# A DeltaNet layer and a multiplicative FFN in one kernel: feature products by 11 of 12 half products, two chunks transposed by TensorE

## The chip, the cores and the metric

One core of a Trainium2 chip runs the whole program. The metric is the device time of one execution in microseconds (us). Engines: TensorE (PE; its weight loads are listed as PEld), VectorE (DVE), ScalarE (ACT), GpSimd (POOL) and SyncE (SP), which issues nearly all transfers.

## What is computed

```
# attention, per (b, h), B=4, H=8, S=768, D=48
k_n = k / (norm(k) + 1e-6);  state = 0
for t in range(S):
    y[t]  = q[t] @ state
    state += beta[t] * outer(k_n[t], v[t] - k_n[t] @ state)
# x: 3072 tokens x 384, the heads side by side
a = x @ w1;  b = x @ w2          # 384 x 1024
out = ((a * b) @ w3) @ w_out     # 1024 x 1024, 1024 x 384
```

The first four inputs are float32. The weights arrive as float64 and are turned into float32 on the chip.

## The kernel before

**Attention.** The sequence is cut into 12 chunks (m) of 64 tokens. For a chunk the kernel loads k, v and q, brings k and q into feature order (`KQ`), forms scores (`scores`, step s), inverts a triangular 64x64 matrix per head from two 32-blocks, updates the state (`chain`, c) and writes the outputs, transposed, into `xT` (`outputs`, y), with six small transfers that move the last head pair's rows into place. Two neighbouring chunks make a pair j. The 32-blocks of a pair are inverted together by `inverse` (V): 31 steps of two DVE operations each, on `V` in PSUM for j < 2 and in SBUF from j = 2 on. `corner` (e) joins the blocks. `squares` (g) and `norms` (N) form the norms of k; their `across` takes a ps_f bank.

**Feature order.** Chunks 0 and 1 are transposed by TensorE (`by_tensor`, steps K and Q, L330, from the token buffers). Chunks 2 to 11 are loaded a second time, in pieces of 32 and 16 features, into `kperm` and `qperm` (`load_perm`, p, L223: 16 transfers each) and transposed by DVE in four operations (`by_vector`, d, L319).

**FFN.** It runs in six units u of 512 tokens, unit u on chunks 2u and 2u+1. First w3 and w_out are folded into `w34` (1024 x 384): `piece` (P, L695) loads a part of a weight into one of five `raw` buffers and turns it into float32 on ACT, DVE and POOL; `transpose_w3` (t) and `fold` (f, L756) do the product. The converted w_out (`wo`, L722) lies in the buffer of w2, so w2 is written after the folds. `ab` (a; b for the first half of unit 0) forms, for one tile of 128 features, x @ w1 and x @ w2 in one ps_f bank each, three matmuls of 512 columns each (L779); ACT copies the first (L791) and DVE multiplies with the second (L795) into a slab. There are ten slabs; a unit needs eight.

**Output.** The product of a unit's slabs (512 x 1024) with w34 is made by 7 instead of 8 block products: `weight_sums` (T) forms sums of blocks of w34 once, in raw buffers it keeps; `slab_sums` (S, L835) forms the sums of token and feature blocks of the slabs in place, on POOL, 16 operations of 128x256; `o` (L851) makes seven products of eight 192-column matmuls each into four ps_f banks named A, D, C, B; `result` (x, L901) adds them on ACT and DVE and stores. In the last unit two of the products go to other banks.

**Order.** `ORDER` lists the steps by name; every function is a generator that runs to its next `yield` when its name comes up. At the end `in_text_order` ties each engine's instructions to that order, so no engine overtakes its own list; between engines only data and buffers make waits. PSUM has four banks ps_f (`bank`) and two double banks ps_w (`two_banks`); both, and most SBUF buffers, are handed out in turn (`in_turn`).

Of the kernel before, what the change touches and what calls it, by code (L numbers as in the profile page):

```python
# [39 lines left out]
beta k0 P0 g0 P13 P10 P0 k1 P18 beta K0 P0 P0 P12 P13 P13 q0 P10 P18 P10 P10 K0 K0 P13 K0 beta  # L40
K0 g0 g0 q1 P8 P1 P18 g0 P12 P18 P12 K1 g0 k2 K1 K1 K1 g0 g0 P12 Q0 K1 Q0 Q0 g0 Q0 g0 P5 g0 N0
Q0 Q1 P8 P8 s0 t5 Q1 Q1 g1 Q1 Q1 s1 g1 s0 P8 g1 P9 s0 s1 s1 s1 s0 t4 t2 s0 p2 P1 P5 s0 s0 s1 s1
V0 P11 P5 P5 N0 P3 t5 P1 P1 d2 u0 P9 d2 u1 P11 P3 P9 P4 P11 N0 P3 t4 P4 P4 P9 P11 t3 t2 P2 P7
P2 P14 t0 P7 P3 P2 V0 V0 t10 P6 s1 P2 P14 t3 V0 P7 V0 V0 V0 P6 f1 g1 p3 P4 P7 t0 P14 P6 P6 P16
V0 V0 P15 V0 V0 V0 f2 V0 t10 P16 P16 f2 P15 f1 V0 f1 P16 P19 V0 V0 p2 t1 V0 P19 P19 V0 V0 f2 f0
P14 t6 t1 f0 f0 V0 P15 V0 P19 V0 v0 P15 t6 s1 P20 d2 V0 P17 P20 P20 t11 V0 P17 t11 d2 V0 t8 t8
P20 V0 k3 g1 g1 V0 g1 f5 P17 t7 V0 P17 V0 P22 P22 f5 V0 t7 V0 f5 v1 n0 V0 f3 V0 V0 s0 f3 P23
P26 V0 g1 f4 d3 t9 V0 t9 V0 d3 f4 P22 P22 f3 t14 P23 P23 P24 P24 P26 p3 t14 d3 f4 P23 n0 P30
P24 P24 s2 V0 p4 e0 g1 g1 t15 t12 f7 t15 f7 t12 f6 P26 P26 N1 e0 e0 s2 s2 P21 d3 e0 P30 e0 e0
s2 f7 s2 P25 e1 s2 c0 P21 e1 e1 e1 c0 n1 s3 P21 P21 N1 s3 y0 y0 P31 N1 s3 s3 s3 P25 P25 s3 n1  # L50
P31 c0 c0 P25 V1 P30 u2 t13 u3 P32 P30 V1 t13 e1 e1 c1 P31 V1 f6 f6 c1 c1 c1 y1 y0 b1 P32 P32
P32 y1 V1 V1 V1 b0 V1 P31 V1 b0 b2 V1 V1 b1 V1 V1 P27 P27 b1 V1 P27 V1 b1 b2 P29 P29 V1 b3 b3
P29 y1 b3 a03 V1 P28 V1 b3 P27 a01 a02 c1 a03 V1 a00 V1 k4 V1 P29 P28 P28 a01 a00 V1 V1 a00 P28
a02 a05 a00 V1 b5 V1 a05 b6 V1 V1 V1 V1 P35 p4 P35 b6 P33 a07 V1 V1 V1 V1 V1 V1 g2 a07 a04 b5
a04 b7 P33 k5 a06 b4 b7 v2 n2 a01 V1 P35 P33 a06 P34 a03 c1 V1 a03 V1 b2 V1 P35 P33 g2 P34 P34
P34 e2 b2 a01 c2 d4 d4 g2 p5 b4 b0 a04 d4 g2 g2 b0 g2 g2 e2 a07 a06 g2 g2 a04 d4 e2 n2 c2 a07
V2 b4 a06 e2 e2 e2 b5 c2 g2 N2 s4 c2 b4 S0 s4 s4 a02 a02 c2 c2 p5 T b5 T y2 b6 y2 d5 T b7 d5 d5
e3 e3 d5 N2 s4 s4 s4 N2 b7 e3 e3 v3 a05 T u4 a05 s5 b6 S0 s5 s5 S0 s5 s5 n3 o0 x0 e3 e3 s5 c3
n3 c3 S0 u5 S0 S0 S0 S0 o0 S0 S0 S0 S0 c3 c3 o0 V2 y3 x0 o0 V2 S0 V2 S0 V2 V2 V2 o0 V2 y3 V2 k6
x0 S0 g3 c3 g3 g3 S0 g3 V2 v4 x0 o0 V2 V2 V2 y3 V2 a10 a10 x0 x0 k7 x0 o0 V2 x0 x0 a17 V2 V2 V2  # L60
V2 x0 V2 V2 V2 a17 V2 V2 a15 V2 V2 a13 a16 V2 V2 v5 V2 a13 p6 V2 a16 V2 a15 V2 g3 V2 a13 g3 a13
p6 x0 a14 c3 a14 V2 e4 d6 a10 a17 a12 e4 e4 e4 g3 g3 c4 a17 g3 d6 a10 a14 d6 a12 n4 n4 c4 e4 g3
e4 e5 n5 a12 c4 a11 d6 N3 a14 c4 c4 n5 a11 y4 p7 p7 c4 e5 s6 a11 s6 s6 y4 a15 a12 a11 c5 e5 V3
a16 d7 d7 d7 d7 o1 c5 v6 a16 k8 g4 g4 e5 g4 p8 a15 g4 s7 s7 S1 e5 s7 S1 e5 x1 s7 s7 S1 s7 c5 o1
s6 S1 u7 c5 o1 s6 s6 u6 S1 S1 V3 S1 y5 c5 c5 V3 V3 V3 V3 V3 o1 S1 x1 k9 S1 y5 S1 y5 o1 S1 S1 x1
x1 V3 S1 S1 V3 c6 V3 S1 S1 V3 d8 o1 x1 x1 v7 a20 n6 x1 V3 a20 o1 x1 a23 V3 V3 x1 V3 x1 n7 a27
a24 d8 a26 V3 V3 V3 V3 x1 g4 V3 a23 V3 a25 V3 a27 a27 V3 a24 V3 V3 a26 a20 V3 g4 V3 p8 V3 V3 V3
V3 p9 V3 V3 a25 d8 n6 d8 g4 a20 a22 a22 a24 V3 c6 a27 a25 a24 a21 a21 e6 e6 e6 g4 e7 N3 e6 a25
N3 g4 s8 g4 N4 s8 e6 a22 s8 a26 e6 c6 c6 N4 s8 a26 s8 y6 a22 V4 p9 N4 S2 d9 e7 s8 a21 e7 y6 u8
d9 a21 e7 c6 a23 d9 p10 e7 d9 S2 c6 S2 s9 n7 a23 s9 e7 o2 s9 c7 s9 S2 s9 k10 S2 c7 x2 o2 c7 S2  # L70
S2 o2 u9 s9 V4 c7 V4 S2 y7 V4 V4 x2 V4 g5 g5 V4 p10 d10 y7 S2 x2 S2 o2 y7 V4 o2 x2 c7 V4 V4 S2
S2 V4 o2 a35 x2 x2 k11 x2 S2 V4 x2 S2 a35 v8 V4 S2 V4 V4 S2 V4 x2 n8 o2 a37 x2 V4 v9 V4 V4 V4
x2 a34 n8 V4 V4 a36 a30 V4 V4 V4 V4 V4 a37 V4 a34 a33 V4 g5 a33 a30 a32 a36 V4 V4 V4 V4 a34 a33
V4 V5 a32 e8 n9 c7 e8 a30 c8 a33 e8 e9 e8 g5 a35 a34 c8 a30 e8 g5 d10 a32 e9 g5 a32 g5 a36 e8
e9 S3 c8 a36 a35 a31 d10 d10 e9 a31 n9 c8 g5 c8 c8 g5 g5 e9 a31 s10 N5 e9 p11 s10 s10 a31 c9
# [14 lines left out]
def kernel(  # L90
# [24 lines left out]
    NT = 2 * B * C  # L115
    assert (B, H, D, DM, NT) == (4, 8, 48, 384, 512) and NCH % 2 == 0

# [74 lines left out]
    kperm, qperm = (padded(x, [P, B, NP, 2, BS], 1)[0] for x in ("kperm", "qperm"))  # L192
# [30 lines left out]
    def load_perm(m):  # L223
        for src, dst in ((k, kperm), (q, qperm)):
            for e in range(2):
                for j in range(2):
                    nd = min(BS, D - BS * j)
                    for tb in range(2):
                        t0 = C * m + BS * tb
                        sync.dma_start(  # L230
                            out=dst[quarter(2 * e + j), :, :, tb, 0:nd].rearrange(
                                "t b a d -> t (b a) d"
                            ),
                            in_=src.rearrange("b (a e) t d -> e (b a) t d", e=2)[
                                e, :, t0 : t0 + BS, BS * j : BS * j + nd
                            ].rearrange("g t d -> t g d"),
                        )
            yield
# [7 lines left out]
    def across(src, dst):  # L246

        n = src.shape[1]
        ps = bank([P, n, NR, NP])
# [3 lines left out]
        psv = ps[:].rearrange("p c r a -> p (c r) a")  # L253
# [10 lines left out]
    def squares(j):  # L264
# [9 lines left out]
        yield from across(ss[:, 1], ss[:, 0])  # L274

    def norms(j):
# [31 lines left out]
        yield from across(w[:, 0], w[:, 1])  # L308
# [10 lines left out]
    def by_vector(m):  # L319
        KQ = new_KQ(m)  # L320
        for i, src in enumerate((kperm, qperm)):
            for z in range(2):
# [3 lines left out]
                    in_=src[:, bs].rearrange("p b a x d -> p (b a) (x d)"),  # L326
# [363 lines left out]
    CW = 512  # L690

    def slab(name):
        return in_turn(ffn, [P, CW], "slab", 10, name)

# [27 lines left out]
    wo = w2s[:].rearrange("p m f -> p (m f)").rearrange("p (j d) -> p j d", d=DM)  # L722

    def piece_wo(j):
        return piece(DM, [(slice(0, P), moe_w_out[j * P : (j + 1) * P, :])], lambda: wo[:, j])
# [30 lines left out]
    def fold(jc):  # L756
        ps = bank([P, CW])
        for kc in range(KF):
            pe.matmul(  # L759
                ps[:, 0:DM], lhsT=w3Ts[jc, kc // 4][:, kc % 4 * P : kc % 4 * P + P],  # L760
                rhs=wo[:, kc], start=(kc == 0), stop=(kc == KF - 1),
# [38 lines left out]
    HB, HF, HD = B // 2, KF // 2, DM // 2  # L800
    ws_ = {}
# [4 lines left out]
    def weight(i):  # L806
        f, d = i
        return w34[:, HF * f : HF * f + HF, d_half(d)]

    def weight_sums():  # L810
# [11 lines left out]
        U3 = room[4][:, 0:DM]  # L822
        ws_.update(T1=B12, T2=T2, T3=T3, T4=T4, B11=B11, B21=B21, B22=B22, M1=M1, U2=U2, U3=U3)
# [10 lines left out]

    def slab_sums(u):  # L835
        for out_, x, y, op in (
# [5 lines left out]
            for i in range(HF):  # L842
                o_, x_, y_ = (
                    abs_[u, HF * f + i][:, tokens(z)] for z, f in (out_, x, y)
                )
                pool.tensor_tensor(out=o_, in0=x_, in1=y_, op=op)  # L846
                yield
# [3 lines left out]
    def o(u):  # L851
        for z, f, w, n, first in (
# [18 lines left out]
            for b in range(HB):  # L871
                t0 = (HB * z + b) * P
                for i in range(HF):
                    pe.matmul(  # L874
                        ps[b][:, b, :], lhsT=abs_[u, HF * f + i][:, t0 : t0 + P],
# [20 lines left out]
    last = NCH // 2 - 1  # L896
# [4 lines left out]
    def result(u):  # L901
# [17 lines left out]
        else:  # L919
            plus("M1", "B")(ws_["U3"])  # L920
            yield
        yield from store(u, 1, 1, plus("U3", "C"))
        yield from store(u, 1, 0, plus("U3", "D", ALU.subtract))
# [6 lines left out]
    def load_k(m, dma=sync.dma_start):  # L930
        ktoks[m] = load_crossed(k, m, dma, "ktok", 4)
# [32 lines left out]
    parts = {"beta": betas_, "T": weight_sums}  # L964
# [11 lines left out]
    for m in range(2):  # L976
# [3 lines left out]
    for j in range(NCH // 2):  # L980
# [3 lines left out]
        for jc in range(KF):  # L984
            parts[f"a{j}{jc}"] = lambda u=j, jc=jc: ab(u, jc, u == 0, 2)
        if j == 0:
            for jc in range(KF):
# [57 lines left out]
```

## Time and profile before

| | us |
|---|---|
| median of 3 runs | 609.24 |
| lowest, highest | 608.55, 610.59 |
| span of the profiled execution | 607.4 |
| PE busy, PEld busy | 550.0, 383.1 |
| DVE, ACT, POOL busy | 364.9, 158.9, 177.2 |

The span is the time from the first to the last instruction of one profiled execution; the runs' times are taken around whole executions. In the groups of the profile a row names line, engine, operation, out<-in by the program's names, shapes and count, then busy us and the mean ns of one, then the idle time ahead and what ended it. A float32 matmul stands as two rows of TensorE, two passes. PEclk is the share of TensorE's clock that was granted. A wait is put down to the last of its releasers.

### The profile page before, as it was taken

How to read it: one execution, taken by the hardware profiler on the slowest of the kernel's cores; microseconds unless marked ns; L12 is line 12 of the kernel's file. 1: busy time of each engine (PE TensorE's matmuls, PEld its weight loads, DVE VectorE, ACT ScalarE, POOL GpSimd, SP SyncE). 2: the span in 40 equal slices, each digit the busy share in tenths (PEclk: the TensorE clock that was granted, in tenths of full speed). 3: DMA queues.
4: the chain of work that ended last, by engine and by line, in shares of the span. 5: the costliest groups of instructions: out<-in, count | busy, mean ns of one | idle time of the engine just before them, and what ended most of it. 6: DMA issues, size and time to landing. Idle time of an engine off the chain costs nothing.

```text
span 607.4 us, 19078 instructions
## 1 busy us (share of the span) xinstructions
PE 550.0 (91%) x8188; PEld 383.1 (63%) x8188; DVE 364.9 (60%) x828; ACT 158.9 (26%) x333; POOL 177.2 (29%) x223
## 2 busy tenths in 40 slices
PE   2648789678898999999999989999999999999997
PEld 2545455657777885456964559745588545984477
DVE  3768977466998489765489463894764843311012
ACT  3645534445323111222111221121112012321100
POOL 6554443122255530304420016013053000600041
PEclk9988979669999999999999999999999999999999
DMA  9968998554956347462443534435323040010001
GB/s 192 244 155 226 186 189 173 97 133 94 165 104 88 82 92 120 92 98 39 101 101 73 81 52 87 97 70 103 58 51 84 31 85 5 5 52 13 1 0 52
DMA packets 219507, 57.31 MB, mean 94 GB/s; under 512 B 206656, under 2 KB 212800, under 8 KB 219424
## 3 DMA queue, kind: packets, MB, share of 16 engines
q1 hardware_dynamic: 215232, 55.31, 45.3%
q10 hardware_dynamic: 4192, 0.79, 0.9%
q8 instruction: 64, 1.05, 0.8%
q14 instruction: 19, 0.16, 0.1%
HBM read 43.88 MB, written 11.01 MB: 90 GB/s over the span
## 4 chain that ended last, share of the span: by engine, by line
PE 75%; DVE 8%; DMA 5%; issue 4%; ACT 3%; SPq 3%; ACTq 0%; DVEq 0%
PE ps_f L779 37%; PE ps_f L874 16%; PE ps_w L551 5%; PE ps_f L759 4%; PE ps_w L652 4%; DMA raw<-in_moe_w_dram 3%; PE ps_w L498 3%; PE ps_w L367 2%; DVE tb L440 2%; PE ps_w L373 2%; SPq L230 2%; DVE ps_w L445 2%; DMA ktok<-in_k_dram 1%; ACT xT L673 1%; PE ps_f L750 1%
## 5 line engine op out<-in xcount | busy, mean ns | idle before, releaser
L779 PE MATMUL ps_f<-xT,w2s 128*128 128x512 f32 (+1 forms) x336 | 133.7, 544 | 1.6 <-issue 1.5
L779 PE MATMUL ps_f<-xT,w1s 128*128 128x512 f32 (+1 forms) x336 | 128.7, 533 | 4.5 <-DVE ab L795 2.0
L846 POOL TENSOR_TENSOR ab<-ab 128x256 f32<-128x256 f32 x96 | 67.2, 729 | 195.0 <-DVE ab L795 171.0
L779 PEld LDWEIGHTS ps_f<-xT,w1s 128*128 128x128 f32 x336 | 63.0, 190 | 60.3 <-issue 52.0
L779 PEld LDWEIGHTS ps_f<-xT,w2s 128*128 128x128 f32 x336 | 63.2, 193 | 56.2 <-issue 52.3
L791 ACT COPY ab<-ps_f 128x512 f32<-128x512 f32 (+1 forms) x56 | 28.4, 525 | 172.7 <-PE ps_f L779 161.4
L874 PE MATMUL ps_f<-w,ab 128*128 128x192 f32 x376 | 66.5, 330 | 0.0
L874 PEld LDWEIGHTS ps_f<-w,ab 128*128 128x128 f32 x376 | 61.1, 190 | 4.4 <-issue 3.5
L795 DVE TENSOR_TENSOR ab<-ab,ps_f 128x512 f32<-128x512 f32 (+1 forms) x56 | 33.2, 605 | 49.1 <-PE ps_f L779 49.0
L440 DVE TENSOR_TENSOR tb<-Vb,Ub 128x31 f32<-128x31 f32 (+15 forms) x124 | 46.0, 371 | 15.5 <-DMA Ub<-Ud 12.1
L759 PE MATMUL ps_f<-w2s,w3T 128*128 128x384 f32 x128 | 48.4, 535 | 5.7 <-ACT w3T L753 5.0
L445 DVE TENSOR_TENSOR Vb<-Vb,tb 128x31 f32<-128x31 f32 (+15 forms) x124 | 47.2, 381 | 4.3
L874 PE MATMUL ps_f<-room,ab 128*128 128x192 f32 x272 | 47.9, 330 | 1.1 <-DVE room L905 1.1
L874 PEld LDWEIGHTS ps_f<-room,ab 128*128 128x128 f32 x272 | 44.1, 190 | 1.9 <-issue 1.5
L673 ACT COPY xT<-ps_w 48x256 f32<-48x256 f32 x96 | 30.4, 365 | 48.1 <-PE ps_w L652 47.5
L759 PEld LDWEIGHTS ps_f<-w2s,w3T 128*128 128x128 f32 x128 | 26.2, 211 | 24.2 <-ACT w3T L753 5.5
L270 POOL TENSOR_TENSOR sq<-ktok 128x384 f32<-128x384 f32 x24 | 20.9, 875 | 61.4 <-DMA ktok<-in_k_dram 30.1
L367 PE MATMUL ps_w<-KQ 48*64 48x128 f32 x384 | 31.3, 308 | 3.9 <-issue 2.0
L379 DVE TENSOR_TENSOR U<-ps_w,wt 128x512 f32<-128x512 f32 x24 | 16.6, 690 | 29.9 <-PE ps_w L373 28.6
L715 POOL TENSOR_TENSOR w<-w,raw 128x512 uint32<-128x512 uint32 x16 | 20.7, 1299 | 43.6 <-DVE w L711 18.6
L373 PE MATMUL ps_w<-KQ 48*64 48x64 f32 x768 | 32.1, 242 | 0.3 <-issue 0.3
L537 POOL TENSOR_TENSOR vtok<-vtok,n 128x384 f32<-128x384 f32 x24 | 20.1, 851 | 41.0 <-DMA vtok<-in_v_dram 26.8
(109 smaller groups left out, 676.4 us busy)
## 6 DMA issues: line engine op xcount, KB each, us to landing
raw<-in_moe_w_dram SPq DMA_DIRECT2D x16, 512.0 KB, 6.2
vtok<-in_v_dram SPq DMA_DIRECT2D x24, 192.0 KB, 4.3
raw<-in_moe_w_dram SPq DMA_DIRECT2D x24, 192.0 KB, 4.0
out_dram<-osb SPq DMA_DIRECT2D x46, 96.0 KB, 2.2
ktok<-in_k_dram SPq DMA_DIRECT2D x44, 96.0 KB, 3.9
raw<-in_moe_w_out_dram SPq DMA_DIRECT2D x8, 384.0 KB, 4.8
Ud<-U SPq DMA_DIRECT2D x48, 64.0 KB, 2.1
Ub<-Ud SPq DMA_DIRECT2D x6, 512.0 KB, 3.4
```

Of the source, the lines that this page charges most:

```text
L367: pe.matmul(ps[half(z), 0, n : n + 128], lhsT=x[:, 0, :], rhs=x.rearrange("p j t -> p (j t)"), start=True, stop=True,)
L373: pe.matmul(ps[half(z ^ j), 1, n + C * j : n + C * j + C], lhsT=x[:, 0, :], rhs=x[:, j, :], start=True, stop=True,)
L440: dve.tensor_tensor(out=tv, in0=V[:, 0 : s + 1, s : s + 1].to_broadcast([P, s + 1, n]), in1=U[:, s, s + 1 : BS].unsqueeze(1).to_broadcast( ...
L445: dve.tensor_tensor(out=o, in0=o, in1=tv, op=ALU.subtract)
L551: pe.matmul(out(ps, r, h, z), lhsT=lhs(r, h, z), rhs=rhs(r, h, z), start=True, stop=True,)
L673: act.copy(out=xT[f, p:NP:2, b : b + NR, cc, :].rearrange("p a r t -> p r a t"), in_=pyv[f, z, b : b + NR],)
L759: pe.matmul(ps[:, 0:DM], lhsT=w3Ts[jc, kc // 4][:, kc % 4 * P : kc % 4 * P + P], rhs=wo[:, kc], start=(kc == 0), stop=(kc == KF - 1),)
L779: pe.matmul(ps[:].rearrange("p b c t -> p b (c t)"), lhsT=w[:, m, js], rhs=x[:, m, :, c0:c1].rearrange("p b c t -> p b (c t)"), start=(m = ...
L791: act.copy(out=t, in_=ps)
L795: dve.tensor_tensor(out=t, in0=t, in1=ps, op=ALU.mult)
L846: pool.tensor_tensor(out=o_, in0=x_, in1=y_, op=op)
L874: pe.matmul(ps[b][:, b, :], lhsT=abs_[u, HF * f + i][:, t0 : t0 + P], rhs=ws_[w][:, i], start=first and i == 0 and (b == 0 or n == "F"), s ...
```

## The change

1. **Feature products of units 1 to 5.** The two halves of a unit's 512 tokens are the block rows. Of the 384 inputs, the first two tiles of 128 are the block columns; w1 and w2 are the block columns on the other side. These 2x2x2 block products are made by 7 instead of 8; the third tile of 128 adds its 4 as they are. `features` (steps a1x to a5x, now four a unit, each for two feature tiles) replaces `ab` there and makes the eleven half products in four ps_f banks; `features_sums` (W) forms the weight sums once, `token_sums` (X) the token sums of a unit, partly in the fourth slot of `xT`, partly in a new buffer `extra`. `tmp` and `first` are new single buffers between ACT, POOL and DVE. Slabs hold two feature tiles of one token half; there are nine.
2. **slab_sums** works on these slabs, eight operations of 128x512; in the last unit on DVE.
3. **Chunks 2 and 3** are transposed by TensorE (`range(4)` for `range(2)`); their q is loaded by tokens.
4. **One permuted buffer** `perm` serves k and then q for chunks 4 to 11; the new buffer `more` holds two blocks of w_out and later a weight sum.
5. **w_out** lies in the second `xT` buffer (five blocks), in `more` (two) and in `tmp` (one).
6. `ktok` has three buffers instead of four; `across` takes ps_w from pair 2 on; `result` keeps a sum in M1 instead of U3 except in the last unit.
7. **ORDER** is new, 1595 steps for 1317. The feature steps of unit 2 and their surroundings, before and after:

```
 before: ... a20 ... a23 V3 V3 x1 V3 x1 n7 a27 / a24 d8 a26 V3 V3 V3 V3 x1 g4 V3 a23 V3 a25 ...
 after:  ... x1 x1 n6 n6 a20 V3 V3 X2 X2 / X2 X2 S1 S1 o1 S1 c6 p8 d8 d8 x1 x1 N3 x1 x1 x1 p8 V3 V3 V3 S1 o1 x1 x1
         a20 V3 V3 V3 V3 n7 V3 V3 / n7 N3 V3 V3 a20 a20 a20 ... d8 / c6 a21 a21 a21 ...
```

```diff
-    kperm, qperm = (padded(x, [P, B, NP, 2, BS], 1)[0] for x in ("kperm", "qperm"))
+    perm = padded("perm", [P, B, NP, 2, BS], 1)[0]
+    more = persist.tile([P, 2 * CW], FP32, name="more")
+    tmp, first = (persist.tile([P, 2, C * B], FP32, name=x) for x in ("tmp", "first"))
+    extra = persist.tile([P, C * B], FP32, name="extra")
...
-        return in_turn(ffn, [P, CW], "slab", 10, name)
+        return in_turn(ffn, [P, CW], "slab", 9, name)
...
-    wo = w2s[:].rearrange("p m f -> p (m f)").rearrange("p (j d) -> p j d", d=DM)
+    def wo(j):
...
+            x = in_turn(ffn, [P, NP, B, 2, C], "xT", 2, "wo")
...
+        host, i = (guests[0], j) if j < 5 else (more, j - 5)
+        if j == 7:
+            host, i = tmp[:].rearrange("p j t -> p (j t)"), 0
+        return host[:, DM * i : DM * i + DM]
...
+    def token_sums(u):
+        A11, A12, A21, A22 = (x_of(u, i % 2, i // 2) for i in range(4))
+        S1, S2, S3 = A21, x_of(u, KM, 1), x_of(u, KM, 0)
+        for out_, x, y, op in (
+            (S3, A11, A21, ALU.subtract),
+            (S1, A21, A22, ALU.add),
+            (S2, S1, A11, ALU.subtract),
+            (extra[:], A12, S2, ALU.subtract),
+        ):
+            pool.tensor_tensor(out=out_, in0=x, in1=y, op=op)
+            yield
...
+        def onto(ps, w, x, first=False):
+            for j in range(2):
+                pe.matmul(
+                    ps[:, j, :], lhsT=w[j], rhs=x, start=first and j == 0, stop=j == 1,
+                    skip_group_check=not first,
+                )
...
+        ps_a = new()
+        onto(ps_a, B11, A11, True)
+        yield
+        Y0 = both(slab("y0"))
+        act.copy(out=Y0, in_=ps_a[:])
+        yield
+        ps_b = new()
+        onto(ps_b, T1, S1, True)
+        yield
+        act.copy(out=tmp[:], in_=ps_b[:])
+        yield
+        ps_d = new()
+        onto(ps_d, T2, S2, True)
+        yield
+        dve.tensor_tensor(out=Y0, in0=Y0, in1=ps_d[:], op=ALU.add)
+        yield
+        pool.tensor_tensor(out=tmp[:], in0=tmp[:], in1=Y0, op=ALU.add)
+        yield
+        ps_c = new()
+        onto(ps_c, T3, S3, True)
+        yield
+        Y1 = both(slab("y1"))
+        dve.tensor_tensor(out=Y1, in0=Y0, in1=ps_c[:], op=ALU.add)
+        yield
+        onto(ps_a, B21, A12)
+        yield
+        onto(ps_a, B31, X1)
+        yield
+        act.copy(out=first[:], in_=ps_a[:])
+        yield
+        onto(ps_b, B22, S4)
+        yield
+        onto(ps_b, B32, X1)
+        yield
+        dve.tensor_tensor(out=Y0, in0=Y0, in1=ps_b[:], op=ALU.add)
+        yield
+        pool.tensor_tensor(out=Y0, in0=Y0, in1=first[:], op=ALU.mult)
+        yield
+        onto(ps_d, T4, A22, True)
+        yield
+        onto(ps_d, B31, X2)
+        yield
+        dve.tensor_tensor(out=Y1, in0=Y1, in1=ps_d[:], op=ALU.add)
+        yield
+        onto(ps_c, B32, X2)
+        yield
+        dve.tensor_tensor(out=tmp[:], in0=tmp[:], in1=ps_c[:], op=ALU.add)
+        yield
+        pool.tensor_tensor(out=Y1, in0=Y1, in1=tmp[:], op=ALU.mult)
+        abs_[u, p, 0], abs_[u, p, 1] = Y0, Y1
+        yield
...
-                pool.tensor_tensor(out=o_, in0=x_, in1=y_, op=op)
+                (dve if u == last else pool).tensor_tensor(out=o_, in0=x_, in1=y_, op=op)
...
-    for m in range(2):
+    for m in range(4):
         parts[f"q{m}"] = lambda m=m: load_q(m, act.dma_start if m == 0 else sync.dma_start)
```

## The prediction, before the changed kernel was run

> **What bounds the kernel now.** I read the page first, parts 1, 2 and 4.
>
> ```profile
> span 607.4 us, 19078 instructions
> PE 550.0 (91%) x8188; PEld 383.1 (63%) x8188; DVE 364.9 (60%) x828; ACT 158.9 (26%) x333; POOL 177.2 (29%) x223
> PE   2648789678898999999999989999999999999997
> DVE  3768977466998489765489463894764843311012
> PEclk9988979669999999999999999999999999999999
> DMA  9968998554956347462443534435323040010001
> PE ps_f L779 37%; PE ps_f L874 16%; PE ps_w L551 5%; PE ps_f L759 4%; PE ps_w L652 4%; DMA raw<-in_moe_w_dram 3%; PE ps_w L498 3%; PE ps_w L367 2%; DVE tb L440 2%; PE ps_w L373 2%; SPq L230 2%; DVE ps_w L445 2%; DMA ktok<-in_k_dram 1%; ACT xT L673 1%; PE ps_f L750 1%
> ```
>
> Two regimes: up to about slice 9 no engine is full, DMA is busiest and the clock falls; afterwards PE is full. The chain that ended last is PE for 75%, the feature products (L779) alone 37%. So I asked the windows view for seven stretches, cut at unit 0's first product and at the last product of each unit's o step (columns: stretch, its length, busy time of PE, PEld, DVE, ACT, POOL, PEclk, DMA share, GB/s).
>
> ```profile
> 0.00:139.30 139.30, 98.41 (x1565) 71.15 (x1565) 93.09 (x202) 65.51 (x122) 59.69 (x68) 0.87 0.81 177
> 139.30:232.30 93.00, 86.20 (x1471) 73.44 (x1472) 73.45 (x179) 27.59 (x66) 37.10 (x45) 0.98 0.54 102
> 232.30:313.30 81.00, 79.33 (x1366) 53.09 (x1365) 54.77 (x122) 15.27 (x34) 19.99 (x28) 1.00 0.53 92
> 313.30:393.80 80.50, 77.81 (x1245) 51.32 (x1244) 52.91 (x128) 15.36 (x34) 16.77 (x24) 1.00 0.44 76
> 393.80:472.70 78.90, 78.66 (x1305) 52.03 (x1304) 51.30 (x120) 15.18 (x34) 21.35 (x29) 1.00 0.39 76
> 472.70:546.50 73.80, 72.75 (x1042) 47.07 (x1041) 30.33 (x64) 15.08 (x34) 11.18 (x16) 1.00 0.14 35
> 546.50:607.40 60.90, 56.86 (x203) 35.04 (x201) 9.08 (x16) 4.96 (x9) 11.10 (x16) 1.00 0.05 16
> ```
>
> In the last five PE works 365.4 of 375.1 us; 4.1 of the idle 9.7 is the tail after the last product. What PE saves there is saved, if nothing else becomes late. In the first stretch 41 us of PE lie idle.
>
> **Part 1, the products of units 1-5.** A matmul stands as two passes. From the chain and the PE timeline:
>
> ```profile
> 546.54 38.62 PE ps_f L779 x90
> 585.16 13.00 PE ps_f L874 x80
> 143.21 1.46 PE L779 MATMUL ps_f<-xT,w2s 128*128 128x256 f32 x6
> 144.51 1.46 PE L779 MATMUL ps_f<-xT,w1s 128*128 128x256 f32 x6
> 145.80 1.46 PE L779 MATMUL ps_f<-xT,w2s 128*128 128x256 f32 x6
> ```
>
> A 512-wide pass takes 38.62/90 = 0.429 us. At 256 wide six passes start 1.295 apart, 0.216 a pass; at 192 wide 0.1625. Two feature tiles now cost 12 matmuls x 2 x 0.429 = 10.30 us; after, 11 half products x 2 matmuls x 2 x 0.216 = 9.50. Saved: 0.80 x 20 pairs = **16.0 us of PE**. Weight loads rise from 24 to 44 a pair, 190 ns each = 8.4 us; they stay hidden, since in the 192-wide stretch one stands behind every 162 ns pass (they overlap each other). The Trainium skill (Perfetto Trace Analysis, Matmuls) says that larger matmuls are more efficient than smaller ones, which speaks against halving them; here the half-width pass costs 50.3% of a full one, so by the rows the penalty is 0.06 us a pair, and that is in the sum. If halving cost the whole saving, the sum below would be 16 higher, 608.
>
> **Part 2, what the saved product costs elsewhere**, per pair of tiles. DVE: five 128x512 operations with a PSUM operand for two (row L795, 682 ns): +2.05 us, +41 in all. POOL: three 128x512 operations of SBUF (row L393, 1276 ns): +3.8, +77 in all. ACT: three copies for two (587 ns), +12 in all. Once a unit POOL forms token sums, 4 x 0.73 = 2.9; once, weight sums, 6 x 1.28 + 4 x 0.73 = 10.6. Slab sums become 8 x 1.28 = 10.2 for 16 x 0.73 = 11.7 in units 1-4; in unit 5 eight move to DVE, about 0.69 each = 5.5. DVE ends near 405 us, POOL near 263, so neither is full by its sum. Stretch by stretch, counting what stands between the same marks in the new order at before's durations: PE 73.9 in unit 0 (72.8 by the same count before), then 74.7, 74.7, 73.5, 69.1, 58.0 = 350.0 for units 1-5 (before 365.4); DVE 86, 67, 58, 52, 38 for units 0 to 4. DVE has room from unit 2 on; in units 0 and 1 it has little.
>
> **Part 3, the hand-overs.** One pair uses all four ps_f banks. In the new PE order the tightest are d and c: DVE must have read the bank within two half products, 1.73 us; one read is 0.68 plus about 0.2 of signalling. So a pair runs dense when DVE is free and misses when a longer operation stands ahead (R, S: 0.95). Between the sixth and seventh product of an o step two DVE operations (2 x 0.55, with signals 1.5) stood behind a 2.57 us feature product; after, behind 0.86: 0.65 late, each unit. A missed wait costs about 0.3, as at 176.6 to 178.1, where four passes took 1.46 instead of 0.86 over two waits. I take 2.6 us a unit, 13 for five, from 0 (all hidden) to 35 (every second half product misses: 5.5 x 0.3 x 20 = 33). One spare slab instead of two, and single tmp, first and extra: tmp passes DVE, POOL and ACT (0.9 + 1.4 + 0.8 = 3.1) while PE does five half products (4.3); hidden. The copy that waits there holds ACT's queue, with y's copies and the corners' behind it, for which only the chunks wait. Units 1-5 then are 350.0 + 4.1 + 13 = 367 for 375.1: **-8**.
>
> **Part 4, the head.** Chunks 2 and 3: four groups of 64 passes, 1.95 to 2.4 us each (L337), +8.8 on PE, in its 41 idle us; if that cover were gone, +8.8 on the path. DVE loses eight transposes (0.69) and gains four copies (0.67): -2.8; ACT +12 x 0.58. SP loses 32 issues of about 0.62 and gains 4. Each chunk's 8192 small packets (16 transfers of 32 x 16 rows) become 2048 for q's tokens (k's are loaded either way); at the mean of part 3 (45.3% x 607.4 x 16 / 215232 = 20.5 ns, on 16 engines) that is 10.5 us for 2.6, at most 16 for both, of 113 busy. The q loads go to token buffers that Q0 and Q1 have freed; k3 now waits for chunk 0's state product and holds SP, but stands behind that product in the order. w_out in xT frees w2s for w2 before the folds end; w2's first half landed in time anyway (no idle before the first L779 on w2s), so 0. One buffer for k and q makes q's loads wait for k's transposes; SP already waited 12.8 us on such (L230 on DVE), the bound here is another 12.8, of which I take 0, since two chunks' worth has gone.
> The chain: k, scores, V0 (31 steps of DVE), corner 0, chunks 0 and 1, first product at 139.3. V0 began at 52.7, 14 us after the last U, its load standing on SP behind chunk 2's k; 28 us of DVE work stood ahead of it, after 23. It ended at 84.9, but corner 0's transpose came at 104.0, behind norms, w1 and w3 pieces; after, six w3 pieces (6.7 us) stand there. What was pushed back (norms, scores, 17 us) now stands between chunks 0 and 1. To the end of chunk 1 DVE has 98 us for 106. I take **-9** for the first stretch, between 0 and -18 (V0 10 earlier, 8 less work). Unit 0 keeps its 93: PE unchanged, DVE 86 of it.
>
> **The sum.** 130.3 + 93 + 367 = 590.3 against the span of 607.4. The median of the runs, 609.24, is 1.8 above that span; 590.3 + 1.8 = **592**.
>
> **Rivals.**
> A, DVE shut out by POOL. In the timeline around the end of unit 1 (start, length, engine, operation):
>
> ```profile
> 311.90 0.41 DVE L445 TENSOR_TENSOR Vb<-Vb,tb 128x240 f32<-128x240 f32 x1
> 312.70 0.83 POOL L537 TENSOR_TENSOR vtok<-vtok,n 128x384 f32<-128x384 f32 x1 [14.20 <-DMA out_dram<-osb]
> 312.80 1.00 DVE L445 TENSOR_TENSOR Vb<-Vb,tb 128x247 f32<-128x247 f32 x1
> ```
>
> With both inputs in SBUF, DVE ended only after POOL did; L795, which reads PSUM, stays at 0.68. V2 to V5 are 248 such operations, and in the new order they stand in the o phases beside slab sums, token sums and v's scaling: 8 x 1.28 + 4 x 0.73 + 2 x 0.85 = 14.9 us a unit. DVE's room is 7 us in unit 0 and 8 in unit 1, then 17 and 22: 8 + 7 = 15 us late, 592 + 15 = 607, from 600. For it: DVE's load; against: before, 24 of the 248 were lengthened, by 0.35 us on the mean, 8 us, since POOL was mostly done first. The Trainium skill (GPSIMD Engine Reference, Key points) has the two sharing SBUF interfaces for DVE instructions with two SBUF inputs; the rows agree. Chance 0.17.
> B, the other side: the banks. If DVE, behind 0.4 to 0.95 us of other work, misses d, c and four more of the eleven hand-overs, each costs 0.3 plus about 0.2 waited: 6 x 0.5 x 20 = 60 us of PE instead of 13, 592 + 47 = 639; it decides from 3 misses a pair (30 us, 609) on, so 611 to 640. For it: every bank is in use, and 20 pairs have no fifth. Against: covers of 1.7 us and more. The Trainium skill (TensorE: Matmul & The Clock Gate, A second HAM failure mode) says that cycling through PSUM with small idles can drop the clock as well; here the clock stayed at 1.00 through the last five stretches. Chance 0.22.
> C, the head gains nothing (another chain, raw loads or DVE's order, is as late): 592 + 9 = 601. Chance 0.08.
> D, the head gains all 18 and the hand-overs cost nothing: 592 - 9 - 13 = 570, half way 581. Chance 0.13.
> That the change does not do what it says: the instruction counts show 440 half-width products for 240, so I leave it out.
>
> **How the numbers follow.** The forecast (585 to 600) has 0.40. Faster by over 0.3%, about what a measurement of this kernel can tell from no change: 0.40 + D 0.13 + C 0.08 + 0.10 of A = 0.71; within: 0.07 of A; slower: B, 0.22. The range 582 to 616 leaves out about 0.06 of D and 0.12 of B.
>
> **What would show it.** Right: L779's successors at 0.216 a pass in runs of many; stretches of 77 to 79 us for units 1 and 2; first unit-0 product near 130; L465 at its 0.4. Wrong: PE idle before feature products on DVE's y or tmp (B); L460 and L465 near 1 us in the o phases (A); DVE above 95% in units 0 and 1, so that they do not shorten.

## The result, and the profile after

The changed kernel takes 659.17 us (median of 4 runs, 654.25 to 661.5) beside 608.89 for the kernel before (605.83 to 610.59). The ratio is 1.083, 95% interval 1.078 to 1.088: **slower by 8%**, where 592 was forecast and 616 was the upper end. The profiled execution took 654.25 us, the least of the four; its stretches below account for 45 of the 50 us.

The page of the changed kernel, parts 1, 2 and 4:

```profile
span 652.3 us, 20578 instructions
PE 556.6 (85%) x8844; PEld 472.6 (72%) x8844; DVE 457.9 (70%) x892; ACT 177.9 (27%) x365; POOL 263.0 (40%) x264
DVE  2789966788777898668987487985586796403352
PEclk9857998798995979999969998999999899999999
PE ps_f L920 20%; DVE tb L460 9%; PE ps_f L1028 9%; DVE Vb L465 8%; PE ps_f L807 4%; PE ps_w L571 4%; DMA raw<-in_moe_w_dram 2%; PE ps_w L518 2%; PE ps_w L672 2%; PE ps_w L387 1%; PE ps_w L393 1%; SPq L717 1%; DVE w L729 1%; DMA ktok<-in_k_dram 1%; PE ps_f L357 1%
```

POOL ends at 263.0 us, as forecast; DVE at 457.9 instead of 405. In the chain stand the two operations of V (L460, L465) with 17% of the span; before, they had 4%. The granted clock dips far behind the head. The windows view, cut at the same marks as before (first unit-0 product, last product of each o step; columns as in the prediction):

```profile
0.00:124.65 124.65, 90.19 (x1489) 64.08 (x1489) 90.71 (x187) 69.97 (x130) 57.28 (x66) 0.84 0.81 180
124.65:248.20 123.55, 103.10 (x1869) 88.43 (x1866) 100.78 (x202) 29.94 (x70) 54.00 (x60) 0.88 0.50 88
248.20:344.07 95.87, 79.01 (x1386) 68.89 (x1385) 76.41 (x143) 17.74 (x38) 36.26 (x34) 0.95 0.42 75
344.07:432.03 87.96, 79.98 (x1385) 70.52 (x1385) 66.83 (x136) 17.74 (x38) 35.79 (x33) 0.96 0.42 76
432.03:517.17 85.14, 77.43 (x1317) 67.66 (x1317) 59.06 (x114) 17.64 (x38) 36.33 (x35) 0.98 0.37 69
517.17:593.04 75.87, 71.48 (x1125) 62.50 (x1125) 40.97 (x75) 17.52 (x38) 28.11 (x24) 1.00 0.14 32
593.04:652.30 59.26, 55.43 (x284) 50.50 (x283) 23.17 (x36) 7.41 (x13) 15.24 (x12) 1.00 0.05 17
```

Against before the head is 14.6 us shorter. Unit 0 is 30.5 longer, unit 1 14.9, unit 2 7.5, unit 3 6.2, unit 4 2.1; unit 5 is 1.6 shorter. The loss shrinks from unit to unit with DVE's load, and unit 5, which has no V beside it, is the only one that gains.

**Where PE waits.** TensorE's timeline in unit 1's o phase (start, length, engine, line, what; in brackets idle time and releaser):

```profile
319.78 2.76 PE L1028 MATMUL ps_f<-room,y 128*128 128x192 f32 x16
322.38 1.03 PE L920 MATMUL ps_f<-xT,w1s 128*128 128x256 f32 x4
335.67 4.23 PE L1028 MATMUL ps_f<-room,y 128*128 128x192 f32 x16 [12.27 <-DVE room L1058]
341.23 2.84 PE L1028 MATMUL ps_f<-w,y 128*128 128x192 f32 x16 [0.17 <-DVE osb L1058]
```

The fifth product (319.78) opens bank B. DVE must read it (L1058) before the sixth adds to it. This read is the fourth step of `result`; outside the lists of the order x3 and x4 stand for the third and fourth step of one unit's result, so the read is called x4. DVE came to it at 334.98:

```profile
334.98 0.55 DVE L1058 TENSOR_TENSOR room<-room,ps_f 128x384 f32<-128x384 f32 x1
```

PE stood for 12.27 us; the sixth product then took 4.23 us instead of 2.8, at half clock. The same wait is 6.50 us in unit 0 (the profile names POOL there, but the product starts 0.15 us after DVE's read ends), 4.26, 4.32 and 0.81 in units 2 to 4: 28.2 us, and 7 more in four products at half clock. In unit 3 DVE itself stood idle for 4.98 us ahead of V5, waiting for a transfer (Ub from Ud), so there the wait is not DVE's work alone. Waits of feature products (L920) come to 6 us in all.

**What DVE does meanwhile.** DVE's timeline at the start of that phase, and POOL's:

```profile
307.82 1.26 DVE L465 TENSOR_TENSOR Vb<-Vb,tb 128x31 f32<-128x31 f32 x1
309.12 1.22 DVE L460 TENSOR_TENSOR tb<-Vb,Ub 128x60 f32<-128x60 f32 x1
311.60 0.25 DVE L460 TENSOR_TENSOR tb<-Vb,Ub 128x87 f32<-128x87 f32 x1
```
```profile
307.77 1.27 POOL L976 TENSOR_TENSOR y<-y,tmp 128x512 f32<-128x512 f32 x1 [2.26 <-DVE tmp L974]
309.00 5.22 POOL L1000 TENSOR_TENSOR y<-y,y 128x512 f32<-128x512 f32 x4
```

A DVE operation on 31 elements a partition takes 1.26 us and ends just after POOL's; the one at 311.60, which slipped in between two of POOL's, takes 0.25. So **about one operation of V passes for each operation of POOL**. Over the run, V2 to V5 take 128.3 us for 93.2.

The o phase of unit 1, first to last product, before and after, in the windows view (columns as above), and of the same windows the larger V row each (busy us, mean ns):

```profile
281.70:313.30 31.60, 30.56 (x648) 27.77 (x647) 19.88 (x45) 5.26 (x13) 11.79 (x17) 1.00 0.43 90
```
```profile
309.30:344.10 34.80, 22.37 (x186) 21.64 (x186) 31.56 (x52) 4.09 (x11) 16.56 (x16) 0.85 0.28 53
```
```profile
L445 DVE TENSOR_TENSOR Vb<-Vb,tb 128x31 f32<-128x31 f32 (+12 forms) x13 | 4.8, 371 | 0.4
```
```profile
L465 DVE TENSOR_TENSOR Vb<-Vb,tb 128x192 f32<-128x192 f32 (+14 forms) x23 | 14.3, 623 | 0.8
```

Before, this phase held 26 operations of V (9.0 us with L440) beside 30.6 us of PE work, a chunk's scores among it. Now it holds 46 of V (28.5 us with L460), and PE has little but o's products. PE's and DVE's work no longer lie side by side.

### The profile page after: what moved, and what is told of

Same layout as the page of the kernel before. It is cut to its first block, busy times and chain, and to the rows that moved or that the text cites. A ratio compares the mean times of both kernels' runs of the same rounds, so it can differ in the third digit from the quotient of the medians.

```text
span 652.3 us, 20578 instructions
## 1 busy us (share of the span) xinstructions
PE 556.6 (85%) x8844; PEld 472.6 (72%) x8844; DVE 457.9 (70%) x892; ACT 177.9 (27%) x365; POOL 263.0 (40%) x264
## 4 chain that ended last, share of the span: by engine, by line
PE 46%; DVE 30%; issue 7%; DMA 6%; SPq 5%; ACT 3%; POOL 1%; DVEq 0%; POOLq 0%; ACTq 0%
PE ps_f L920 20%; DVE tb L460 9%; PE ps_f L1028 9%; DVE Vb L465 8%; PE ps_f L807 4%; PE ps_w L571 4%; DMA raw<-in_moe_w_dram 2%; PE ps_w L518 2%; PE ps_w L672 2%; PE ps_w L387 1%; PE ps_w L393 1%; SPq L717 1%; DVE w L729 1%; DMA ktok<-in_k_dram 1%; PE ps_f L357 1%
## 5 line engine op out<-in xcount | busy, mean ns | idle before, releaser
L920 PE MATMUL ps_f<-xT,w1s 128*128 128x256 f32 x320 | 79.8, 382 | 0.7 <-DMA xT<-xT 0.7
L465 DVE TENSOR_TENSOR Vb<-Vb,tb 128x31 f32<-128x31 f32 (+15 forms) x124 | 65.7, 530 | 4.3
L460 DVE TENSOR_TENSOR tb<-Vb,Ub 128x31 f32<-128x31 f32 (+15 forms) x124 | 62.6, 505 | 8.2 <-DMA Ub<-Ud 5.0
L920 PEld LDWEIGHTS ps_f<-xT,w1s 128*128 128x128 f32 x320 | 60.0, 190 | 9.0 <-issue 1.0
L920 PE MATMUL ps_f<-xT,w2s 128*128 128x256 f32 x240 | 62.6, 385 | 1.9 <-DVE y L962 1.2
L1028 PE MATMUL ps_f<-room,y 128*128 128x192 f32 x224 | 44.1, 356 | 21.7 <-DVE room L1058 21.7
L1028 PEld LDWEIGHTS ps_f<-room,y 128*128 128x128 f32 x224 | 41.2, 210 | 23.2 <-issue 23.0
L1028 PE MATMUL ps_f<-w,y 128*128 128x192 f32 x312 | 55.8, 335 | 1.2 <-DVE osb L1058 1.2
L1028 PEld LDWEIGHTS ps_f<-w,y 128*128 128x128 f32 x312 | 52.4, 195 | 2.5 <-issue 2.2
L920 PEld LDWEIGHTS ps_f<-xT,w2s 128*128 128x128 f32 x240 | 44.2, 190 | 9.0 <-DVE y L962 2.1
L693 ACT COPY xT<-ps_w 48x256 f32<-48x256 f32 x96 | 30.5, 366 | 59.3 <-PE ps_w L672 58.8
L1000 POOL TENSOR_TENSOR y<-y,y 128x512 f32<-128x512 f32 x32 | 41.3, 1316 | 7.8 <-PE ps_f L1028 7.4
L920 PE MATMUL ps_f<-xT,room 128*128 128x256 f32 x160 | 42.3, 387 | 1.1 <-DVE y L970 1.1
L387 PE MATMUL ps_w<-KQ 48*64 48x128 f32 x384 | 30.6, 310 | 11.8 <-DVE PT L417 9.7
L787 PE MATMUL ps_f<-wo,w3T 128*128 128x384 f32 x80 | 32.9, 556 | 4.0 <-POOL wo L733 3.8
L387 PEld LDWEIGHTS ps_w<-KQ 48*64 48x64 f32 x384 | 25.6, 155 | 14.6 <-issue 11.7
L920 PEld LDWEIGHTS ps_f<-xT,room 128*128 128x128 f32 x160 | 29.2, 190 | 6.7 <-DVE y L970 1.8
L733 POOL TENSOR_TENSOR w<-w,raw 128x512 uint32<-128x512 uint32 x16 | 21.1, 1323 | 30.7 <-DVE w L729 15.9
```

The lines of the kernel that those rows point to most:

```text
L387: pe.matmul(ps[half(z), 0, n : n + 128], lhsT=x[:, 0, :], rhs=x.rearrange("p j t -> p (j t)"), start=True, stop=True,)
L460: dve.tensor_tensor(out=tv, in0=V[:, 0 : s + 1, s : s + 1].to_broadcast([P, s + 1, n]), in1=U[:, s, s + 1 : BS].unsqueeze(1).to_broadcast( ...
L465: dve.tensor_tensor(out=o, in0=o, in1=tv, op=ALU.subtract)
L693: act.copy(out=xT[f, p:NP:2, b : b + NR, cc, :].rearrange("p a r t -> p r a t"), in_=pyv[f, z, b : b + NR],)
L787: pe.matmul(ps[:, 0:DM], lhsT=w3Ts[jc, kc // 4][:, kc % 4 * P : kc % 4 * P + P], rhs=wo(kc), start=(kc == 0), stop=(kc == KF - 1),)
L920: pe.matmul(ps[:, j, :], lhsT=w[j], rhs=x, start=first and j == 0, stop=j == 1, skip_group_check=not first,)
```

## The experiments

All ratios are to the kernel before, run beside them; the changed kernel itself stands at 1.083. Two theories stood against each other at first. **Lock-out**: POOL makes DVE's SBUF operations slow, and DVE's list is late. **Order**: x4 stands behind V in DVE's list, and that alone is the price.

**e1, result first** (unit 1 shown; units 0 to 4 alike):

```diff
-... x1 o1 x1 v6 o1 S1 k8 S1 o1 V3 V3 V3 V3 V3 y5 V3 v7 V3 V3 V3 x1 x1 n6 n6 a20 ... o1 ... x1 x1 N3 x1 x1 x1 ...
+... o1 x1 x1 x1 v6 o1 S1 k8 S1 o1 x1 V3 V3 V3 V3 V3 y5 V3 v7 V3 V3 V3 n6 n6 a20 ... o1 x1 x1 x1 ...
```

> Only the order differs from the changed kernel: in units 0 to 4 the result's steps (x) stand directly behind the product whose bank they read, so that DVE reads bank B after the fifth product of o ahead of the V steps that stood between. Order theory (the result's read stands behind V2 to V4 in DVE's list, and the sixth product waits for it): PE's waits of L1028 for DVE room L1058 and POOL vtok L557, 28.2 us in all, fall under 6, and with the half-clock stretches behind them the time falls by 25 to 32, to about 630. Lock-out theory (DVE is slow because POOL shuts out its SBUF-to-SBUF operations; the order only decides who pays): V2 to V5 keep their lengthened operations and what follows them (corners, transposes) is late instead; at most 10 us faster, 649 or more.

The copy of bank A into M1 also came to stand behind the third product, so that M1 holds another sum; the amount of work is the same. Measured: 669.96 us, 1.100 (1.094 to 1.106), **slower still**, so the order theory falls. The waits moved on: to unit 1's first y (5.58 us behind DVE's y L942), to xT (10.8 in three waits, SP's transfers), to osb (8.01 in unit 2). What stands behind V in DVE's list waits for V; for xT the trace names only the transfers.

**e2, short slab sums**

```diff
+                    if u < last:
+                        o_, x_, y_ = (w[:, :, 0:8] for w in (o_, x_, y_))
```

> The changed kernel in its own order, but in units 1 to 4 each of POOL's eight slab sums takes 8 of 512 columns; the rest of the sums is left out. Lock-out theory: each slab sum of 1.27 us held one DVE operation of V for about 0.85 longer, 6.8 us a unit; V3 then reaches the result's step about 7 us earlier, the 12.3 us wait in unit 1's o falls to about 5 and the 4.3 in unit 2 goes: 643 to 648. Order theory: the 47 V operations ahead of the result's read in unit 1 set the wait by their number; it stays at 9 or more, 653 to 657. Unit 0 keeps its 6.5 us wait and its 6.4 us wait for PT in both.

632.48 us, 1.040 (1.036 to 1.044): 26 us back, more than either theory gave. V2 to V5 fall to 108.5 us, unit 1's wait to 4.41.

**e3, weight sums early** (POOL only)

```diff
-a03 P34 b7 b7 a06 b5 g2 g2 a03 T g2 ... s5 T T T c3 n3
+a03 P34 b7 b7 a06 b5 g2 g2 a03 T T T T g2 ... s5 c3 n3
```

> Only POOL's order differs from the changed kernel: the last six of the eight block sums of w34 (L860, 1.01 us each) stand directly behind the first two, ahead of the squares of chunk 5, which wait for k; POOL is idle there (175 to 188 us). Lock-out theory: the eight norm operations at 191 to 199 us go from 0.92 to 0.19 us, PT's wait of 6.4 us falls to about 1 and the stretch at half clock behind it (210 to 224 us) gets shorter: 648 to 652. Rival (the load of chunk 5's k into one of three buffers sets the time there, the norms being late in any case): 656 or more.

649.45 us, 1.068 (1.064 to 1.072), as lock-out has it. The second operation of the norms, in the changed kernel and in e3 (DVE's timeline):

```profile
193.30 0.93 DVE L309 TENSOR_TENSOR nt<-nt,seed 128x32 f32<-128x32 f32 x1
```
```profile
192.47 0.19 DVE L309 TENSOR_TENSOR nt<-nt,seed 128x32 f32<-128x32 f32 x1
```

**e4, both orders** (the edits of e1 and e3, M1 as in e1)

> The two changes of order together (result's steps first, weight sums early). Order theory: the gains add, 25 to 32 and 7 to 11, 618 to 628, still slower than the kernel before if unit 0's second half and units 1 and 2 keep DVE's lengthened operations. Lock-out theory with the order of no account: 640 or more.

664.37 us, 1.092 (1.088 to 1.096): e1's loss and about half of e3's gain (all of it would give 1.085). The order theory is out; of lock-out only the bound (640 or more) holds, since the order does count, the wrong way.

From here on a third theory is asked, the **DVE list**: DVE has more listed ahead of the reads that PE needs than PE has products, so the amount of DVE's work counts, and moving a single read only moves the wait.

**e5, only the first sum early** (on e3's order; units 0 to 2)

```diff
-... x1 o1 x1 v6 o1 S1 k8 S1 o1 V3 V3 V3 V3 V3 y5 V3 v7 V3 V3 V3 x1 x1 n6 n6 a20 ...
+... x1 o1 x1 v6 o1 S1 k8 S1 o1 x1 x1 V3 V3 V3 V3 V3 y5 V3 v7 V3 V3 V3 n6 n6 a20 ...
```

> e3's kernel (weight sums early, 649.5 us) and in units 0 to 2 only the two steps of the result that end in the read of bank B (x3, x4) directly behind o's fifth product, the rest of the result where it was. Order theory: the sixth product's waits for L1058 (31.2 us in all in e3) fall under 10: about 630. DVE-list theory (what was seen in e1: whatever stands in DVE's list behind V waits for V in the end, the seventh product or the next unit's first y): the wait moves on, 645 to 651.

660.72 us, 1.086 (1.082 to 1.090), 11 slower than e3; the range of 645 to 651 missed this as well. In unit 1 the one wait of 11.97 us before the sixth product became two, before the sixth and the seventh:

```profile
327.58 5.48 PE L1028 MATMUL ps_f<-room,y 128*128 128x192 f32 x16 [5.15 <-POOL y L1000]
340.44 5.46 PE L1028 MATMUL ps_f<-w,y 128*128 128x192 f32 x16 [6.21 <-DVE osb L1058]
```

The sum is nearly the same, 11.4 us, and now two products run at half clock; DVE also idles 2.8 us ahead of x4, waiting for the fifth product. Only the second wait is for DVE's list. The first is for a slab sum, which comes late in e5: it stands in POOL's list behind token sums, and these waited 8.3 us for xT's transfers (0.9 in the changed kernel).

**e6, slab sums on DVE**

```diff
-                (dve if u == last else pool).tensor_tensor(out=o_, in0=x_, in1=y_, op=op)
+                (dve if u else pool).tensor_tensor(out=o_, in0=x_, in1=y_, op=op)
```

> The changed kernel (659.2 us) with the slab sums of units 1 to 4 on DVE, as unit 5 has them, in the same places of the order. Lock-out theory: POOL's eight sums held one DVE operation each for 0.85 us, 6.8 a unit; on DVE they take about 0.66 each, 5.3 a unit: DVE's list in the o phases gets 1 to 2 us shorter a unit, 649 to 657. Rival (e2 was 27 us faster because the sums themselves come early for o's products): DVE makes them in half of POOL's time, so most of the 27 us come back: 632 to 642.

658.89 us, 1.082 (1.078 to 1.087), nothing gained. V2 to V5 fall by 20.2 us to 108.1, and DVE makes 32 more operations of 0.78 us on the mean, 25 us. DVE's busy time is as long as before (458.6 for 457.9), and so is the time. The rival isn't put to the test by this: on DVE the sums come later, not earlier, since they stand between V's operations, and PE now waits 12.5 us for them, 8.15 of it before unit 1's sixth product. What speaks against it is the changed kernel's own trace, in which no product waits for a slab sum.

**e7, three orders** (e5 and e6 together)

> e5 and e6 together: weight sums early, the read of bank B first, slab sums on DVE. DVE-list theory: about the gain of e3 and a few us, 640 to 650. Order theory: 618 to 632.

663.92 us, 1.093 (1.088 to 1.099): outside both, on the side of the DVE list.

**h1, half of V**

```diff
+            if j >= 2 and s % 2:
+                yield
+                continue
             t = in_turn(work, [P, 256], "tb", 2, "tb")
```

> The changed kernel (659.2 us), in its own order, with every second of the 31 steps of V2 to V5 left out; POOL's work stays. DVE-list theory (in the o phases of units 0 to 3 DVE has more listed ahead of the reads that PE needs than PE has products; V, lengthened by POOL, is most of it): about 15 us of DVE a unit go, the 12.3, 7.6 and 4.3 us waits go, and the half-clock stretches behind them: 615 to 628. Rival (half-width products, their banks or the clock cost by themselves what was lost): 645 or more.

621.87 us, 1.023 (1.018 to 1.029), as the DVE-list theory has it.

**h2, the kernel before with more V**

```diff
-            dve.tensor_tensor(
+            for _ in range(1 if j < 2 else 2):
+                dve.tensor_tensor(
```

> The kernel before with the first of the two operations of each step of V2 to V5 issued twice: 124 more DVE operations of about 0.37 us, 46 us in all, nearly 11.5 us a unit in units 0 to 3, as much as POOL's lock-out adds to V in the changed kernel. DVE-list theory: before's order holds V back behind the result's reads only in part and its units have 7 to 28 us of DVE room, so 5 to 25 us slower (612 to 634), most of it in units 0 and 1. If DVE's time were of no account in the o phases: within 3 us of before.

648.14 us, 1.068 (1.062 to 1.074), more than expected: V2 to V5 rise by 43.2 us (93.2 to 136.4) and the time by 40.9. **The kernel before had no room on DVE**, though DVE was busy for 60% of its span. Not units 0 and 1 pay most, as expected: unit 0 is 2.3 us longer, units 1 to 3 9 to 11 each, unit 4 6.8.

**h3, no slab sums** (e3's order; e2's cut in unit 0 too)

> e3's kernel (weight sums early, 649.5 us) with the slab sums of units 0 to 4 cut to 8 of 512 columns (unit 0: 8 of 256); the rest of them is left out. Lock-out theory: the gain of e2 (27 us) adds to e3's, and S0's 16 operations held V2's for about 0.33 each, 5 us more: 615 to 622. If the gains overlap (one wait that was counted twice): 625 to 635.

628.38 us, 1.035 (1.027 to 1.042), between the two figures: by the ratios 29 us below the changed kernel, where e2 and e3 had 26 and 9; the gains overlap.

**h4 and h5, DVE relieved in both kernels** (h1's and h3's cuts; in h5 the same two cuts in the kernel before)

> h3's kernel (weight sums early, slab sums of units 0 to 4 cut to 8 columns) and h1's cut together: every second step of V2 to V5 left out too. If DVE's list is all that holds the changed kernel back, the five units fall to their own PE work: unit 0 about 105, units 1 to 5 about 81, 79, 77, 73, 59, behind a head of 123: 595 to 600, and some 5 to 10 below the kernel before with the same cuts (h5). If half products lose their saving elsewhere (entry into each unit, banks, clock): 600 to 612, no better than h5.

> The kernel before with the same cuts: every second step of V2 to V5 and all but 8 columns of the slab sums of units 0 to 4 left out. PE is full in its units 2 and 3 (78.7 of 78.9 us), so little can be gained there; unit 0 has 7 us, units 1 and 2 have 4: 597 to 604. It is the other side of h4's comparison: h4 below h5 by 5 to 10 us shows PE's saving, h4 at or above h5 shows that it isn't there even with DVE free.

h4: 611.42 us, 1.0006 (0.998 to 1.004). h5: 609.04 us, 1.0000 (0.998 to 1.002). Relief of DVE brings back all 50 us; but h4 is no better than h5, and the kernel before gains nothing from the same relief: more work on DVE costs there (h2), less saves nothing. Units 0, 3 and 4 in the windows view, h4 and then h5:

```profile
123.53:236.13 112.60, 100.35 (x1868) 84.62 (x1866) 82.31 (x182) 29.89 (x70) 41.24 (x56) 0.94 0.55 98
403.17:480.39 77.22, 75.35 (x1317) 66.08 (x1317) 47.22 (x94) 17.59 (x38) 28.09 (x35) 1.00 0.41 76
480.39:554.53 74.14, 70.91 (x1125) 62.90 (x1125) 34.45 (x57) 17.50 (x38) 19.84 (x24) 1.00 0.14 33
```
```profile
138.95:231.99 93.04, 87.67 (x1477) 74.48 (x1472) 66.34 (x165) 27.68 (x66) 29.13 (x45) 0.96 0.56 106
392.82:472.11 79.29, 78.72 (x1305) 52.06 (x1305) 42.16 (x92) 15.17 (x34) 13.31 (x29) 1.00 0.39 76
472.11:545.94 73.83, 72.78 (x1041) 47.10 (x1041) 23.73 (x45) 15.08 (x34) 3.00 (x16) 1.00 0.14 32
```

In units 3 and 4 PE's busy time falls by 3.4 and 1.9 us, but its idle time rises from 1.6 to 5.1 us, so 1.8 of the 6.4 us counted for them are left. The rest of the balance is elsewhere: in h4's trace the head is 15.4 us shorter than in h5's, unit 0 is 19.6 longer, unit 1 1.0 longer and unit 2 5.2 longer. Unit 0 has no half products of features; in unit 2 PE's clock fell to half after idle times of 1.6 and 1.9 us. So h4 shows that no gain is left, but not that half products alone cost it.

**h6, the kernel before with more POOL**

```diff
+            if j >= 2 and s % 2 == 0:
+                pool.tensor_tensor(
+                    out=ws_["spare"], in0=w1s[:, 0, 0:256], in1=w1s[:, 1, 0:256], op=ALU.add
+                )
```

> The kernel before, with 16 further POOL operations (sums of two SBUF tiles, 128x256, 0.73 us) beside every second step of each of V2 to V5, writing to a spare buffer that nobody reads: 11.7 us of POOL a unit, POOL about 35% busy in all. Lock-out theory: each holds one DVE operation of V for about 0.35 longer, 5.6 us a unit, and by h2 (46 us of DVE cost 41) most of that ends on the path: 12 to 25 us slower. Rival (POOL is on nobody's path there and DVE slips between): within 4 us.

624.76 us, 1.025 (1.021 to 1.029). No result of these 64 operations is used (the profile names one of them for a 2.3 us wait of PE in unit 0, but there the product starts 0.15 us after DVE's read of the bank). V2 to V5 still rise by 18.3 us, to 111.5 (of it 55.3 here), and the time by 15.2. By the stretches of the trace, 10.0 lie in unit 3, where V rises by 9.2; units 0 and 2, with 10.0 of V's rise, pay 3.4:

```profile
L445 DVE TENSOR_TENSOR Vb<-Vb,tb 128x31 f32<-128x31 f32 (+15 forms) x124 | 55.3, 446 | 4.3
```

**g1 and g2, half products in the last unit only.** The kernel before with `features`, the sums and the slab format for unit 5 alone; in g2 the two half products without a token sum come first in its first pair:

```diff
+        if p == 0:
+            onto(ps_a, B21, A12)
...
+            onto(ps_a, B31, X1)
...
         ps_b = new()
         onto(ps_b, T1, S1, True)
```

> The kernel before with one thing taken over: unit 5's features by half products, and the sums this needs (its token sums on DVE, the weight sums and slab sums too); units 1 to 4, the slabs' number, ktok, kperm and qperm, chunks 2 and 3 and the order up to unit 5 stay. The buffers that it needs lie in kperm, qperm and a token buffer that are free by then. No V stands beside it. If the saving on PE is real where DVE and POOL are free: 4 pairs x 0.80 = 3.2 us, less up to 1 for the sums, 0.4 to 0.5% faster, about 604.5. If half products cost what they save, or the hand-overs of banks cost 0.3 us a few times a pair: within 0.2% of before.

> g1 with one exchange: in unit 5's first pair the two half products that need no sums (B21 x A12, B31 x X1) stand ahead of the one that needs the second token sum, for which PE waited 1.5 us in g1 behind 0.46 for osb. The saving of 0.216 a pass is then kept: 2 us less than g1, ratio to before 0.994 to 0.997. If a hand-over of ps_a to ACT takes the place of the wait: as g1, 0.998 to 1.002.

g1: 609.43 us, 0.9994 (0.997 to 1.002); g2: 607.51 us, 1.0002 (0.997 to 1.004). No gain that can be measured; neither g1's 0.4 to 0.5% nor g2's 2 us came. From the first product behind the sixth o4 product to unit 5's first o product the profile gives 43.8 us before, 43.1 in g1, 42.6 in g2, 41.4 in the changed kernel: of the 3.2 us counted, 0.7, 1.2 and 2.4 are there. What is missing lies at the entry, where half products need sums of the very chunk that just ended: g1's second half product waits 1.53 us for them (0.46 for osb just ahead); in g2 the first one that needs a sum still waits 1.09.

## Why the prediction was wrong, step by step

- **Part 1, PE's saving: the size of a pass right, the gain overrated.** Half products run at 0.216 us a pass in the changed kernel's unit 5, the last three pairs without a gap. But "saves 0.80 us a pair" holds inside a unit; each unit has its entry to pay: 0.8 us in the changed kernel's unit 5 and 2.5 in g1, of 3.2. Even with DVE relieved no gain is left in the whole (h4 beside h5).
- **Part 2, the step that failed: "DVE has room from unit 2 on; in units 0 and 1 it has little".** The room was taken as the stretch's length less DVE's busy time. DVE's work is of use to PE only in the order of its list, and the new order puts 46 of V's 62 operations into unit 1's o phase, where PE has 22 us of work. h2 measured what DVE's time in V costs: 0.95 us each, in a kernel whose DVE was 60% busy; h6 gives 0.83, both on the mean of the units. POOL's counted total was right; DVE's was 53 below, 35 of it V's lengthening (and its own terms, 364.9 + 41 + 5.5 - 2.8, give 408.6, not 405).
- **Rival A, the right mechanism at a third of its price.** It was priced at 15 us and 607. The slab sums alone cost 26 us (e2), the weight sums beside the norms 9 (e3), together 29 (h3); V's lengthening of 35 us at the 0.83 to 0.95 of h6 and h2 gives 29 to 33. It set DVE's room against the price; there was none. The other 20 came back with half of V (h4). I put them down to DVE's added work, which V stood in for there; that is argued, for no run took the added operations themselves away. That only 24 of 248 operations were lengthened before spoke for the old order, in which POOL was done first, and not for the new one.
- **Part 3, the banks: right for the features, wrong for o.** Feature products wait 6 us in all, within the 13. Between the sixth and seventh product 0.65 us late was forecast, each unit; before the seventh PE waited 0.16 to 0.92. What is late stands before the sixth: 0.81 in unit 4, but 4.3 to 12.3 where V stands ahead of x4 in DVE's list. Those operations were not counted. **Rival B** came out at the time forecast for it or beyond, but not by its mechanism.
- **Part 4, the head: gained, and given back.** The first unit-0 product comes at 124.65, earlier than the 130.3 forecast. Unit 0 did not "keep its 93: PE unchanged": it took 123.55, and to the end of o0 it is 248.2 us for 232.3. PE's passes between the marks rose from 1471 to 1869, mostly the small products of chunks, which used to stand ahead of the first unit-0 product; PE's busy time there is 103.1 us for 86.2, and with DVE relieved still 100.4 for 87.7 (h4, h5). The count had 73.9 for 72.8. So part of the earlier first product is work that moved behind the mark. Of the 15.9 us, the norms beside the weight sums and what follows from them make about 4.5 (e3's o0 ends 5.1 earlier, of which 0.6 stood before its norms); the 6.5 us before the sixth product, and the half clock behind it, are seen in the trace. **Rival C** holds in effect, and more.
- What would show it: L920 at 0.216 was there; 77 to 79 us for units 1 and 2 were not (95.9, 88.0). L460 and L465 near 1 us in the o phases was rival A's sign: 0.62 on the mean in unit 1's.

Open: that the new order's bunching of V is itself part of the loss is seen in the two traces, not shown by a run; an order that spreads V over the feature products again was not tried. How the remaining loss of unit 0 (and in h4 of unit 2) divides between one permuted buffer, three ktok buffers and the order was not separated.

## What to carry to other kernels

Room on an engine is counted phase by phase, between the points where another engine waits for its list, and not over a stretch or a span: an engine at 60% can have none, and adding harmless work (h2, h6) measures it. A product saved in a Strassen-like scheme pays only where the sums it needs are ready and the additions land on an engine with room. Moving one read ahead in a list that is too long moves the wait, and can split it into two.

## What the runs showed of the hardware

- In these traces a DVE operation with both inputs in SBUF that was held beside a POOL operation ended 0.05 to 0.28 us after it (63 lengthened operations of V in the changed kernel), however small: 0.93 us for 32 elements a partition beside a 1.0 us sum, 0.19 alone. The Trainium skill (GPSIMD Engine Reference, Key points) has the two sharing their SBUF interfaces for just such operations; the trace agrees, and shows the wait lasting until POOL's operation ends. V on PSUM (V0, V1) kept its 21.3 us.
- After PE waits of 3.75 us and more, products of o ran at half speed (4.23 to 5.49 us for 2.84); after 2.41 us (e1) one took 2.84. The Trainium skill (TensorE: Matmul & The Clock Gate, HAM oscillation — how this bites in real kernels) puts the gap that does this above about 3.4 us; these waits agree. Others do not: after 3.09 us in h6 a product took 4.44, and in the changed kernel one took 4.55 (at 403.27) after an idle time of 1.87 us just ahead. So the traces set no threshold. Behind the waits of 3.75 us and more it cost another 1.4 to 2.65 us on the next product.
